# h and y of the later expert tiles on ScalarE alone, in an attention, expert and MLP kernel

## The chip, the cores and the metric

The kernel runs on one core of a Trainium2 chip. The metric is the device time of one execution in microseconds (us); of the kernel before, three runs are shown. One more execution was taken by the hardware profiler. Engines are named as in its rows: PE is TensorE (matmuls; PEld its weight loads), DVE is VectorE, ACT is ScalarE, POOL is GpSimd, SP is SyncE, which here issues DMAs. A name with a q (SPq, DVEq) is that engine's queue: instructions that issue DMAs, branch, or handle semaphores.

## The reference

Three stages follow one another, all in fp32: attention with a gated memory, a layer of eight experts of which each token takes one, and a dense MLP.

```python
def reference(...):                 # B,H,S,D = 4,8,576,64
    attn_out = g * mem_out + (1 - g) * softmax(q k^T / 8, causal) v
    x = attn_out.transpose(0, 2, 1, 3).reshape(B * S, H * D)      # 2304 x 512
    # experts: N,D,E,F = 2304,512,8,1024
    logits = x @ w_gate
    expert_idx = np.argmax(logits, axis=1)
    gate_w = softmax(logits)[arange(N), expert_idx]
    for e in range(E):
        mask = expert_idx == e
        h = np.maximum(x[mask] @ w1[e], 0.0)
        out[mask] = gate_w[mask, None] * (h @ w2[e])
    # dense MLP: 512 -> 2048 -> 512
    h = out @ w_in
    g = np.where(h > 0.0, h, np.exp(np.minimum(h, 0.0)) - 1.0)
    return g @ w_out
```

## The kernel before, in words

Every fp32 operand of a matmul is split into a high part (rounded to fp32r) and a low part (the rest); a product is three matmuls, high by high, low by high and high by low. So beside PE's work there is splitting work: a cast makes the high part, a subtraction the low part.

The stage that the change touches is the experts'. Tokens are sorted by expert into tiles of 128, and `mtile(t)` in `moe()` makes one tile. 23 tiles run (t = 0 to 22; two more stand behind an If and are not run here). The first four (`NE`) are made before the last batch of attention is routed; the tiles from t = 4 on are the ones that run one behind the other, with nothing of the attention beside them, from about 272 us to 517 us.

One tile does the following. POOL gathers the tokens (L1165). PE turns them (L1269), ACT and DVE split them (`split()`, high part L1190 on ACT or L1193 on DVE, low part L1196 on DVE). SP loads the expert's weights as four pieces of 1 MB (L1151), into one of two sets of buffers (`wraw` for even tiles, `wrbw` for odd ones); if the tile has the same expert as the tile that used that set before, an If skips load and split. `wsplit(k)` splits piece k: two casts of 128x1024 on ACT (`fh`, L1305) and two subtractions on DVE (`fl`, L1310). Pieces 0 and 1 are the first weight (names `wq` and `ws`), pieces 2 and 3 the second (`w`). 24 matmuls (L1330) make two halves of x w1 in two PSUM buffers. Then h = relu of the two halves: the first half on ACT (L1340), the second on ACT or DVE (L1343), as the setting `"re": [("ACT",), ("ACT", "DVE")]` allows. PE turns each half of h (L1355), ACT makes the high part of each turned half (`hh`, L1190), DVE the low part (`hl`, L1196). 24 matmuls (L1373) make y, and y times the gate is made on ACT (L1386) or DVE (L1389). POOL scatters y's rows to DRAM (L1415).

PE's order in one cycle is: the 24 L1330 of tile t, the turns of tile t+1's tokens (L1269), the turns of the first half of h of tile t (L1355), three L1373 of tile t-1, the turns of the second half, 21 L1373 of tile t-1, and then the L1330 of tile t+1. In the text a tile's cycle is counted from its first L1340 to that of the next tile.

Beside the tiles a piece of the MLP's preparation runs: the two dense weights are packed in 32 parts to a shorter form and stored in DRAM (`Widen.part`). A part is a load of 512 KB by SP into one of two `wide` buffers (L1102 or L1104), an absolute value on ACT (L1109), four packing steps on DVE (L1113, L1117, L1121, L1125), and a store to `wf` by SP (L1129). The load of part n+2 needs the buffer of part n, that is its L1125. The first piece that the MLP needs is read back from `wf` into the same `wide` buffers (L1431) and split there (high part on ACT, `raw0n<-wide`, low part on DVE).

The order on every engine's queue is set by a list scheduler (`Plan`, L116 to 258): each `pl.op(engines, costs, functions, r=..., w=..., prio=...)` is an operation with the keys that it reads and writes, and where two engines are given, the scheduler takes one of them by a table of costs and priorities. It simulates the engines with these costs, so another set of allowed engines or a further key moves operations that aren't named in the diff. What runs on the chip is then a fixed queue for each engine, in which an instruction that waits holds up all behind it.

Of the kernel before, what the change touches and what calls it, by code (L numbers as in the profile page):

```python
# [34 lines left out]
NE = 4  # L35
# [15 lines left out]
BOTH = ("DVE", "POOL")  # L51
# [437 lines left out]
def ca(n, sb=False, bias=False, acc=False):  # L489
    if acc:  # L490
        return 240 + 0.833 * n
    return (110 if sb else 65) + 0.833 * n


def cv(n):
    return 70 + 1.04 * n


def cv2(n):
    return 75 + 0.52 * n  # L500
# [6 lines left out]
def cpt(n):  # L507
    return 150 + 2.1 * n
# [660 lines left out]
def first_parts(c):  # L1169

    nc, pl, K = c.nc, c.pl, c.K
    wx, pr = Slot(c.rx), K["first"]

    def f():
        for cc in range(4):
            nc.tensor.transpose(wx.t[:, cc * P:(cc + 1) * P], c.ex[:, cc:DM:4], c.ident)
    pl.op("PE", 436, f, r=[c.se], w=[wx], prio=pr)
    xh, xl = [t.rearrange("p c n -> p (c n)") for t in c.x0]
    split(c, lambda: wx.t[:, 0:512], lambda: xh, lambda: xl, 512, [wx], "x0h", "x0l", pr, True, ("ACT", "DVE"), ("DVE",))
    for q in range(len(c.wq)):  # L1180
        hi, lo = c.wq[q]
        split(c, lambda q=q: c.wraw[0][0][:, 1024 * q:1024 * (q + 1)], lambda hi=hi: hi, lambda lo=lo: lo, 1024, [("raw", 0, 0)], ("hi", q), ("lo", q),
              pr + 10.0 * q, False, ("ACT", "DVE"), ("DVE",))


def split(c, src, hi, lo, n, rd, wh, wl, pr, psum, eh, el):
    nc, pl = c.nc, c.pl

    def ha():
        nc.scalar.copy(hi(), src())  # L1190

    def hv():
        nc.vector.tensor_copy(hi(), src())  # L1193

    def lv():
        nc.vector.tensor_sub(lo(), src(), hi().bitcast(F32))  # L1196

    def lp():
        nc.gpsimd.tensor_sub(lo(), src(), hi().bitcast(F32))
    he = {"ACT": (ca(n, sb=not psum), ha), "DVE": (cv(n) if psum else cv2(n), hv)}  # L1200
    le = {"DVE": (cv(n), lv), "POOL": (cpt(n), lp)}
    for es, d, r, w in ((eh, he, rd, wh), (el, le, rd + [wh], wl)):
        pl.op(es, [d[x][0] for x in es], [d[x][1] for x in es], r=r, w=[w], prio=pr, share=() if psum else BOTH)


def moe(tc, c, w1, w2, tiles):
    nc = tc.nc
    mp, pl, K = c.mp, c.pl, c.K
# [35 lines left out]
    def mtile(t):  # L1244
        pr = 1000.0 * t

        def at(x, y):
            return pr + y + K["moff"].get(f"{x}{t}", 0.0)
        rw = t % 2 if t < NTM else 1
        raw = c.wraw[rw]  # L1250
        part = t >= NE
        sg = Slot(r_xg)
# [21 lines left out]
        for _ in range(t > 0):  # L1274
            split(c, lambda: wx.t, lambda: xh.t.rearrange("p c n -> p (c n)"), lambda: xl.t.rearrange("p c n -> p (c n)"), 512,
                  [wx], xh, xl, at("xe", K["m_x"]), True, K["xe"], ("DVE",))

        flags = {}
        for e, eng in (("ACT", mybir.EngineType.Activation), ("DVE", mybir.EngineType.DVE)) if t else ():
            def mk(e, eng):  # L1280
                n = t - NE if part else t

                def f():
                    flags[e] = nc.values_load(c.R.sw[part][0:1, 1, n:n + 1], engines=[eng], min_val=0, max_val=1,
                                              skip_runtime_bounds_check_because="made on the chip as a flag")
                pl.op(e, 450, f, r=[("sw", part)], w=[("flag", e, t)], prio=at("f" + e, K["m_fl"]))
            mk(e, eng)

        def wsplit(k, pr):

            def src(q):
                return raw[k][:, 1024 * q:1024 * (q + 1)]
            keys = [[(x, 2 * k + q) for q in range(2)] for x in ("hi", "lo")]
            if not t:
                for q in range(2):
                    n = 2 * k + q
                    if n < len(c.wq):
                        continue
                    split(c, lambda q=q: src(q), lambda n=n: whi[n], lambda n=n: wlo[n], 1024, [("raw", rw, k)], keys[0][q], keys[1][q], at(f"w{n}t", pr - 1000.0 * t), False, K["wh"][n], K["wl"][n])
                return  # L1300

            def fh():
                with tc.If(flags["ACT"] < 1):
                    for q in range(2):
                        nc.scalar.copy(whi[2 * k + q], src(q))  # L1305

            def fl():
                with tc.If(flags["DVE"] < 1):
                    for q in range(2):
                        nc.vector.tensor_sub(wlo[2 * k + q], src(q), whi[2 * k + q].bitcast(F32))  # L1310
            ci = K["same"].get(t, (K["m_if"], K["m_if"]))
            pl.op("ACT", ci[0], fh, r=[("flag", "ACT", t), ("raw", rw, k)], w=keys[0], prio=at(f"sh{k}t", pr - 1000.0 * t))
            pl.op("DVE", ci[1], fl, r=[("flag", "DVE", t), ("raw", rw, k)] + keys[0], w=keys[1], prio=at(f"sl{k}t", pr - 1000.0 * t))

        def wparts(n):
# [2 lines left out]
        for cc in range(4):  # L1318
            def mk(cc):
                p1 = at("1t", K["m_1"] + 10 * cc)  # L1320
                if cc % 2 == 0:
                    wsplit(cc // 2, p1)
                (wh, wl), wk = wparts(cc)

                def mm(hfs, ns):
                    def f():
                        for hf in hfs:
                            for n in ns:
                                a, b = ((xh, wh), (xl, wh), (xh, wl))[n]
                                nc.tensor.matmul(g[hf].t, a.t[:, cc, :], b[:, 512 * hf:512 * (hf + 1)],  # L1330
                                                 start=(cc == 0 and n == 0), stop=(cc == 3 and n == 2))
                    return f
                for hf in range(2):
                    pl.op("PE", 3 * 216, mm((hf,), (0, 1, 2)), r=[xh, xl, *wk], w=[g[hf], ("tile", t)], prio=p1)
            mk(cc)
        sh = Slot(r_h)
        for hf in range(2):
            def mk(hf):
                def fa():
                    nc.scalar.activation(sh.t[:, 512 * hf:512 * (hf + 1)], g[hf].t, AF.Relu)  # L1340

                def fv():
                    nc.vector.tensor_scalar_max(sh.t[:, 512 * hf:512 * (hf + 1)], g[hf].t, 0.0)  # L1343
                es = K["re"][hf]
                pl.op(es, [{"ACT": ca(512), "DVE": cv(512)}[x] for x in es], [{"ACT": fa, "DVE": fv}[x] for x in es], r=[g[hf]], w=[(sh, hf)],
                      prio=at(f"r{hf}t", K["m_h"]))
            mk(hf)
        hs = []
        for k in range(2):
            def mk(k):  # L1350
                wt, hh, hl = Slot(rt), Slot(r_hh), Slot(r_hl)

                def f():
                    for j in range(4):
                        nc.tensor.transpose(wt.t[:, j * P:(j + 1) * P], sh.t[:, (4 * k + j) * P:(4 * k + j + 1) * P], c.ident)  # L1355
                pl.op("PE", 436, f, r=[(sh, k)], w=[wt], prio=at(f"h{k}t", K["m_h"]))
                split(c, lambda: wt.t, lambda: hh.t.rearrange("p c n -> p (c n)"), lambda: hl.t.rearrange("p c n -> p (c n)"), 512,
                      [wt], hh, hl, at(f"he{k}t", K["m_h"]), True, K["he"], ("DVE",))
                hs.append((hh, hl))
            mk(k)  # L1360

        y, sy = Slot(rg if t == NTM - 1 else ry), Slot(Ring("last", [c.wraw[0][0][:, 2 * XW:3 * XW]]) if t == NTM - 1 else r_y)
# [24 lines left out]

        def fv():
            nc.vector.tensor_scalar_mul(sy.t[:, 0:DM], y.t, sg.t[:, DM:DM + 1])  # L1389
        pl.op(("ACT", "DVE"), (ca(512), cv(512)), (fa, fv), r=[y, sg], w=[sy], prio=at("yt", 500))  # L1390

        if t < NE - NY:
            def f():
# [3 lines left out]
        if t < NE:  # L1397
            wy = Slot(rt)
            n = P * (t - NE + NY)
# [20 lines left out]
    for t in tiles:  # L1420
        mtile(t)
# [365 lines left out]
```

## Time and profile before

| | us |
|---|---|
| median of 3 runs | 928.09 (927.58 to 928.56) |
| profiled execution | 929.22 |
| its span, first to last instruction | 927.5 |
| PE busy | 894.7 (96%) |
| DVE busy | 601.5 (65%) |
| ACT busy | 372.0 (40%) |
| mean granted clock of PE | 0.989 |

The span is what the trace covers; the profiled execution's own time is 1.7 us longer. Busy times of the engines overlap. The page also cuts the span into 40 slices with the busy share of each engine in tenths; the experts' tiles stand in the slices 12 to 22, and PE's digit there is 9 in all but one. The clock of PE in that row is the share of full speed that was granted.

### The profile page before, as it was taken

To read this page: it belongs to the slowest core of one execution; us is meant where nothing else is said; L and a number is where in the kernel's file an instruction comes from. 1 tells how busy PE (TensorE), PEld (TensorE's weight loads), DVE (VectorE), ACT (ScalarE), POOL (GpSimd) and SP (SyncE) were. 2 spreads that over 40 slices of the span, in tenths; PEclk is the share of its full clock that TensorE was granted. 3 is DMA by queue.
4 is the path that set the end of the run, shared out by engine and by line. 5 is a ranking of instruction groups with operands and counts; after the bars stand their busy time and mean duration, and the time that the engine had idled before them with its cause. 6 is when DMAs were issued, how large, how long until landed. Compare 5 with 4: busy or idle time off the path is not lost. (4 is left out here: it accounts for less than half of the span.)

```text
span 927.5 us, 19069 instructions
## 1 busy us (share of the span) xinstructions
PE 894.7 (96%) x7404; PEld 742.9 (80%) x7404; DVE 601.5 (65%) x1093; ACT 372.0 (40%) x745; POOL 122.1 (13%) x176
## 2 busy tenths in 40 slices
PE   7999999999999999999989999999999999999996
PEld 4777778777788878887777899988888888888895
DVE  4889898989755787589996784444444444434442
ACT  5677777876432454246663431111111111111110
POOL 1111111121001132222221100010001000100100
PEclk9999999999999999999998999999999999999998
DMA  5444343357436964799984540110011000100000
GB/s 115 91 94 127 70 130 71 102 199 231 144 120 210 321 229 145 256 303 335 308 293 162 190 159 2 46 45 1 12 35 46 1 23 12 46 1 1 25 22 23
DMA packets 97108, 110.04 MB, mean 119 GB/s; under 512 B 65390, under 2 KB 65390, under 8 KB 94704
## 3 DMA queue, kind: packets, MB, share of 16 engines
q1 hardware_dynamic: 90992, 95.26, 32.5%
q0 software_dynamic: 4800, 13.18, 4.2%
q8 instruction: 59, 0.97, 0.4%
q10 hardware_dynamic: 1216, 0.30, 0.1%
q14 instruction: 41, 0.34, 0.1%
HBM read 87.94 MB, written 23.41 MB: 120 GB/s over the span
## 5 line engine op out<-in xcount | busy, mean ns | idle before, releaser
L1582 ACT ACTIVATE elu<-ptt 128x512 f32<-128x512 f32 x72 | 42.9, 597 | 316.5 <-PE ptt L1574 316.5
L1586 DVE TENSOR_SCALAR elu<-elu 128x512 f32<-128x512 f32 x72 | 31.0, 430 | 188.9 <-ACT elu L1582 188.9
L1599 PE MATMUL ptt<-w,gh 128*128 128x512 f32 x432 | 134.7, 393 | 0.0
L1373 PE MATMUL pmt<-w,hh 128*128 128x512 f32 x368 | 126.7, 406 | 0.0
L703 ACT ACTIVATE a<-pat,st 128x128 f32<-128x128 f32 (+3 forms) x144 | 78.0, 547 | 34.6 <-DVE st L698 27.3
L1599 PEld LDWEIGHTS ptt<-w,gh 128*128 128x128 f32 x432 | 79.3, 188 | 15.2
L1599 PE MATMUL ptt<-w,gl 128*128 128x512 f32 x216 | 84.2, 390 | 0.0
L1373 PEld LDWEIGHTS pmt<-w,hh 128*128 128x128 f32 x368 | 70.2, 191 | 14.0 <-DVE w L1310 0.3
L1373 PE MATMUL pmt<-w,hl 128*128 128x512 f32 x184 | 72.6, 394 | 0.0
L1574 PE MATMUL ptt<-yTh,w 128*128 128x256 f32 (+1 forms) x288 | 68.8, 318 | 0.0
L698 DVE TENSOR_REDUCE st<-pat 128x2 f32<-128x256 f32 (+4 forms) x80 | 64.4, 807 | 3.1 <-PE pat L690 1.4
L1488 DVE TENSOR_TENSOR gl<-tnh,gh 128x512 fp32r<-128x512 f32 x72 | 49.9, 693 | 4.7
L1590 DVE SCALAR_TENSOR_TENSOR tnh<-ptt,elu 128x512 f32<-128x512 f32 x72 | 49.8, 692 | 4.2
L820 POOL TENSOR_TENSOR raw<-ms,ls 128x80 f32<-128x80 f32 (+2 forms) x45 | 30.2, 694 | 169.1 <-DVE ls L808 161.7
L1574 PEld LDWEIGHTS ptt<-yTh,w 128*128 128x128 f32 x288 | 49.2, 190 | 3.9
L1599 PEld LDWEIGHTS ptt<-w,gl 128*128 128x128 f32 x216 | 40.5, 188 | 8.7
L676 PE MATMUL pat<-ab 64*128 64x128 f32 (+3 forms) x256 | 46.9, 474 | 0.0
L1574 PE MATMUL ptt<-yTl,w 128*128 128x256 f32 (+1 forms) x144 | 45.8, 318 | 0.0
L113 PE MATMUL pat<-ident,a 64*128 64x64 f32 x800 | 38.0, 233 | 7.1 <-ACT a L703 2.7
L1190 ACT CAST hh<-pmt 128x512 fp32r<-128x512 f32 x46 | 27.1, 589 | 43.4 <-PE pmt L1373 35.9
L1340 ACT ACTIVATE h<-pmt 128x512 f32<-128x512 f32 x29 | 17.3, 598 | 63.2 <-PE pmt L1330 61.6
L113 PEld LDWEIGHTS pat<-ident,a 64*128 64x128 f32 x800 | 30.6, 141 | 12.6 <-ACT a L703 5.9
(345 smaller groups left out, 1962.2 us busy)
## 6 DMA issues: line engine op xcount, KB each, us to landing
wraw<-in_moe_w_dram SPq DMA_DIRECT2D x24, 1024.0 KB
wrbw<-in_moe_w_dram SPq DMA_DIRECT2D x12, 1024.0 KB
wide<-in_moe_w_in_dram SPq DMA_DIRECT2D x16, 512.0 KB
wf<-half SPq DMA_DIRECT2D x32, 256.0 KB
wide<-in_moe_w_out_dram SPq DMA_DIRECT2D x16, 512.0 KB
wide<-wf SPq DMA_DIRECT2D x9, 512.0 KB
v<-in_v_dram SPq DMA_DIRECT2D x32, 128.0 KB
wraw<-yd SPq DMA_DIRECT2D x14, 258.0 KB
```

Of the source, the lines that this page charges most:

```text
L113: nc.tensor.transpose(out, x, ident[hs, hs])
L676: nc.tensor.matmul(s.t[:, 512 * h:512 * h + n], row(1)[hs, i * P:(i + 1) * P], row(0)[hs, 0:n], start=True, stop=False)
L698: nc.vector.tensor_reduce(ss.t[:, 2 * i:2 * i + (2 if i < 4 else 1)], src(), axis=AX.X if i < 4 else AX.XY, op=ALU.min)
L703: nc.scalar.activation(sa[i].t[:, h, :] if i < 4 else sa[4].t[:, 0:S].rearrange("p (y n) -> p y n", y=2), src()[:, h, :] if i < 4 else src ...
L820: e.tensor_tensor(o, a, b, op=ALU.add)
L1373: nc.tensor.matmul(y.t, a.t[:, 2 * (q % 2) + jj, :], b[:, 512 * jj:512 * (jj + 1)], start=(q == 0 and jj == 0 and n == 0), stop=(q == 3 an ...
L1488: nc.vector.tensor_sub(lo(), src(), hi().bitcast(F32))
L1574: nc.tensor.matmul(h.t[:, n * j + n0:n * j + n1], w(cc, a, ft), b(cc), start=(cc == 0 and x == 0), stop=(cc == 3 and x == 2))
L1582: nc.scalar.activation(se.t, h.t, AF.Exp)
L1586: nc.vector.tensor_scalar(se.t, se.t, 1.0, -1.0, op0=ALU.min, op1=ALU.add)
L1590: nc.vector.scalar_tensor_tensor(st.t, h.t, 0.0, se.t, op0=ALU.max, op1=ALU.add)
L1599: nc.tensor.matmul(acc[a].t, y.t[:, n * j + P * a:n * j + P * (a + 1)], wsub(1, k, ft // 2)[:, ft % 2, :], start=(ft == 0 and x == 0), sto ...
```

## The change

Three edits, all for the tiles from the fifth on (t >= NE = 4):

- both halves of h may be made by ACT only (before: the second half by ACT or DVE);
- y may be made by ACT only (before: ACT or DVE);
- the high parts of the turned halves write a further key ("he", k, t), and the ACT split of the second weight piece (`ws`, k = 1) of tile t reads the key of tile t-1's first half, so that the scheduler puts it behind that copy in ACT's queue.

`split()` takes the further keys as its argument `also`.

```diff
--- before.py
+++ after.py
@@ -1183,7 +1183,7 @@
               pr + 10.0 * q, False, ("ACT", "DVE"), ("DVE",))
 
 
-def split(c, src, hi, lo, n, rd, wh, wl, pr, psum, eh, el):
+def split(c, src, hi, lo, n, rd, wh, wl, pr, psum, eh, el, also=()):
     nc, pl = c.nc, c.pl
 
     def ha():
@@ -1199,8 +1199,8 @@
         nc.gpsimd.tensor_sub(lo(), src(), hi().bitcast(F32))
     he = {"ACT": (ca(n, sb=not psum), ha), "DVE": (cv(n) if psum else cv2(n), hv)}
     le = {"DVE": (cv(n), lv), "POOL": (cpt(n), lp)}
-    for es, d, r, w in ((eh, he, rd, wh), (el, le, rd + [wh], wl)):
-        pl.op(es, [d[x][0] for x in es], [d[x][1] for x in es], r=r, w=[w], prio=pr, share=() if psum else BOTH)
+    for es, d, r, w in ((eh, he, rd, [wh, *also]), (el, le, rd + [wh], [wl])):
+        pl.op(es, [d[x][0] for x in es], [d[x][1] for x in es], r=r, w=w, prio=pr, share=() if psum else BOTH)
 
 
 def moe(tc, c, w1, w2, tiles):
@@ -1309,7 +1309,7 @@
                     for q in range(2):
                         nc.vector.tensor_sub(wlo[2 * k + q], src(q), whi[2 * k + q].bitcast(F32))
             ci = K["same"].get(t, (K["m_if"], K["m_if"]))
-            pl.op("ACT", ci[0], fh, r=[("flag", "ACT", t), ("raw", rw, k)], w=keys[0], prio=at(f"sh{k}t", pr - 1000.0 * t))
+            pl.op("ACT", ci[0], fh, r=[("flag", "ACT", t), ("raw", rw, k)] + ([("he", 0, t - 1)] if k == 1 and t >= NE else []), w=keys[0], prio=at(f"sh{k}t", pr - 1000.0 * t))
             pl.op("DVE", ci[1], fl, r=[("flag", "DVE", t), ("raw", rw, k)] + keys[0], w=keys[1], prio=at(f"sl{k}t", pr - 1000.0 * t))
 
         def wparts(n):
@@ -1341,7 +1341,7 @@
 
                 def fv():
                     nc.vector.tensor_scalar_max(sh.t[:, 512 * hf:512 * (hf + 1)], g[hf].t, 0.0)
-                es = K["re"][hf]
+                es = K["re"][hf] if t < NE else ("ACT",)
                 pl.op(es, [{"ACT": ca(512), "DVE": cv(512)}[x] for x in es], [{"ACT": fa, "DVE": fv}[x] for x in es], r=[g[hf]], w=[(sh, hf)],
                       prio=at(f"r{hf}t", K["m_h"]))
             mk(hf)
@@ -1355,7 +1355,7 @@
                         nc.tensor.transpose(wt.t[:, j * P:(j + 1) * P], sh.t[:, (4 * k + j) * P:(4 * k + j + 1) * P], c.ident)
                 pl.op("PE", 436, f, r=[(sh, k)], w=[wt], prio=at(f"h{k}t", K["m_h"]))
                 split(c, lambda: wt.t, lambda: hh.t.rearrange("p c n -> p (c n)"), lambda: hl.t.rearrange("p c n -> p (c n)"), 512,
-                      [wt], hh, hl, at(f"he{k}t", K["m_h"]), True, K["he"], ("DVE",))
+                      [wt], hh, hl, at(f"he{k}t", K["m_h"]), True, K["he"], ("DVE",), [("he", k, t)])
                 hs.append((hh, hl))
             mk(k)
 
@@ -1387,7 +1387,8 @@
 
         def fv():
             nc.vector.tensor_scalar_mul(sy.t[:, 0:DM], y.t, sg.t[:, DM:DM + 1])
-        pl.op(("ACT", "DVE"), (ca(512), cv(512)), (fa, fv), r=[y, sg], w=[sy], prio=at("yt", 500))
+        es = ("ACT", "DVE") if t < NE else ("ACT",)
+        pl.op(es, [{"ACT": ca(512), "DVE": cv(512)}[x] for x in es], [{"ACT": fa, "DVE": fv}[x] for x in es], r=[y, sg], w=[sy], prio=at("yt", 500))
 
         if t < NE - NY:
             def f():
```

What the scheduler makes of it is seen in the queues. A first place is tile 21 (h_4053 is its h, wq and ws the pieces of the first weight of tiles 23 and 22, hh and x the high parts of h and of the next tokens). ACT's queue before:

```order
L1305 CAST wq_86<-wraw_77 128x1024
L1305 CAST wq_88<-wraw_77 128x1024
L1303 UNCONDITIONAL_BRANCH x2
L1109 ACTIVATE half<-wide_72 128x512
L1308 UNCONDITIONAL_BRANCH
L1340 ACTIVATE h_4053<-pmt_4152 128x512
L1303 COMPARE_AND_BRANCH
L1305 CAST ws_4167<-wraw_78 128x1024
```

DVE's queue before at the same place, up to the second half of h:

```order
L1310 TENSOR_TENSOR wq_87<-wraw_77,wq_86 128x1024
L1310 TENSOR_TENSOR wq_89<-wraw_77,wq_88 128x1024
L1308 UNCONDITIONAL_BRANCH x2
L1121 SCALAR_TENSOR_TENSOR half<-wide_71,half 128x512
L1113 TENSOR_SCALAR half<-half 128x512
L1125 SCALAR_TENSOR_TENSOR half<-wide_71,half 128x512
L1303 UNCONDITIONAL_BRANCH
L1343 TENSOR_SCALAR h_4053<-pmt_4153 128x512
L1308 COMPARE_AND_BRANCH
```

And ACT's queue now:

```order
L1305 CAST wq_86<-wraw_77 128x1024
L1305 CAST wq_88<-wraw_77 128x1024
L1303 UNCONDITIONAL_BRANCH x2
L1109 ACTIVATE half<-wide_72 128x512
L1308 UNCONDITIONAL_BRANCH
L1340 ACTIVATE h_4053<-pmt_4152 128x512
L1340 ACTIVATE h_4053<-pmt_4153 128x512
L1190 CAST x_84<-pmt_4151 128x512
L1190 CAST hh_4057<-pmt_4156 128x512
L1303 COMPARE_AND_BRANCH
```

Both halves of h now follow each other on ACT, and the second weight piece's casts, which stood between the first half and x, have moved behind the copy of the first turned half. DVE's L1343 is gone from its queue; the L1109 stands directly ahead of h as before, and it belongs to another part.

A second place is ACT's queue ahead of tile 18 (h_4049 is its h; wq the first weight piece of tile 20). Before:

```order
L1305 CAST wq_86<-wrbw_4113 128x1024
L1305 CAST wq_88<-wrbw_4113 128x1024
L1303 UNCONDITIONAL_BRANCH x2
L1109 ACTIVATE half<-wide_72 128x512
L1308 UNCONDITIONAL_BRANCH
L1340 ACTIVATE h_4049<-pmt_4154 128x512
L1303 COMPARE_AND_BRANCH
```

And now:

```order
L1305 CAST wq_86<-wrbw_4113 128x1024
L1305 CAST wq_88<-wrbw_4113 128x1024
L1303 UNCONDITIONAL_BRANCH x2
L1109 ACTIVATE half<-wide_72 128x512
L1308 UNCONDITIONAL_BRANCH
L1109 ACTIVATE half<-wide_71 128x512
L1340 ACTIVATE h_4049<-pmt_4154 128x512
L1340 ACTIVATE h_4049<-pmt_4155 128x512
```

Two L1109, of parts 25 and 26 in both `wide` buffers, now stand between the weight casts and the two halves of h; before it was one, and the second came after tile 18's h. In most other tiles one L1109 (in tile 17's the high part of the piece read back) stands directly ahead of the two halves, and ahead of the second half in tiles 8, 12 and 15. y (L1386) stands on ACT in each cycle between the casts of the third and the fourth weight piece. PE's own order is that of before, except that the turns of the first half stand three L1373 later in tiles 12 and 15; the order after the experts' stage is unchanged.

## Rows read from the trace of the kernel before

**Rows 1.** The page's busy time of each engine: us, share of the span, instructions.

```profile
PE 894.7 (96%) x7404; PEld 742.9 (80%) x7404; DVE 601.5 (65%) x1093; ACT 372.0 (40%) x745; POOL 122.1 (13%) x176
```

**Rows 2.** What PE waits for, 180 to 560 us: us in total, times, longest.

```profile
PE pmt L1355 <- DVE h L1343: 5.4, 2, 3.7
PE pmt L1355 <- DVEq L1308: 5.0, 3, 1.9
```

**Rows 3.** Table by stage: us, busy us of PE, PEld, DVE, ACT, POOL, clock, DMA share, GB/s.

```profile
340.28:354.68 14.40, 12.49 (x61) 10.24 (x60) 13.46 (x19) 7.17 (x10) 6.61 (x5) 1.00 0.44 140
354.68:391.50 36.82, 36.82 (x181) 30.98 (x180) 22.85 (x38) 10.04 (x17) 8.31 (x11) 1.00 0.61 205
...
428.60:442.64 14.04, 12.51 (x61) 10.24 (x60) 12.52 (x15) 9.61 (x13) 6.55 (x5) 1.00 0.89 303
442.64:456.75 14.11, 12.49 (x61) 10.25 (x60) 13.40 (x19) 6.82 (x9) 3.75 (x4) 1.00 0.87 311
...
469.04:483.04 14.00, 12.48 (x61) 10.24 (x60) 12.13 (x17) 9.72 (x13) 5.05 (x4) 1.00 0.66 221
...
483.04:501.81 18.77, 15.03 (x61) 12.19 (x60) 15.85 (x23) 5.77 (x8) 3.24 (x5) 0.82 0.72 250
```

**Rows 4.** Timeline of tile 21: start us, us, engine, line, operation, wait before it.

```profile
483.04 0.60 ACT L1340 ACTIVATE h<-pmt 128x512 f32<-128x512 f32 x1
...
484.48 2.36 DVE L1310 TENSOR_TENSOR wq<-wraw,wq 128x1024 fp32r<-128x1024 f32 x2
...
488.29 0.68 DVE L1343 TENSOR_SCALAR h<-pmt 128x512 f32<-128x512 f32 x1
...
489.03 1.11 PE L1355 MATMUL pmt<-ident,h 128*128 128x128 f32 x4 [3.74 <-DVE h L1343]
...
489.80 0.78 PE L1373 MATMUL pmt<-w,hh 128*128 128x512 f32 x1
...
496.85 2.88 PE L1330 MATMUL pmt<-wq,x 128*128 128x512 f32 x12
```

**Rows 5.** Timeline of PE in tile 10: first and next after its 21 second matmuls.

```profile
344.86 0.47 PE L1373 MATMUL pmt<-w,hh 128*128 128x512 f32 x1
...
349.72 0.39 PE L1330 MATMUL pmt<-wq,xh 128*128 128x512 f32 x1
```

**Rows 6.** Groups by line, 267 to 517 us: busy us, mean ns, idle before.

```profile
L1340 ACT ACTIVATE h<-pmt 128x512 f32<-128x512 f32 x21 | 12.5, 598 | 54.6 <-PE pmt L1330 53.2 <-issue 1.2
...
L1343 DVE TENSOR_SCALAR h<-pmt 128x512 f32<-128x512 f32 x17 | 11.7, 690 | 19.9 <-PE pmt L1330 19.0 <-DVEq L1308 0.5
...
L1386 ACT ACTIVATE wraw<-pmt,xs 128x512 f32<-128x512 f32 x1 | 0.7, 687 | 3.0 <-PE pmt L1373 3.0
...
L1109 ACT ACTIVATE half<-wide 128x512 f32<-128x512 f32 x30 | 20.2, 678 | 8.7 <-DMA wide<-in_moe_w_in_dram 4.5 <-DMA wide<-in_moe_w_out_dram 2.3 <-ACTq L1303 1.8
```

**Rows 7.** Timeline of tile 11, where ACT makes both halves of h.

```profile
354.68 1.31 ACT L1340 ACTIVATE h<-pmt 128x512 f32<-128x512 f32 x2 [2.54 <-PE pmt L1330]
...
355.64 0.60 PE L1355 MATMUL pmt<-ident,h 128*128 128x128 f32 x4
```

**Rows 8.** Timeline: loads into wide, the steps that waited, and the read-back's low part.

```profile
357.27 1.68 SPq L1104 DMA_DIRECT2D wide<-in_moe_w_out_dram  x1
...
362.36 0.67 ACT L1109 ACTIVATE half<-wide 128x512 f32<-128x512 f32 x1 [2.30 <-DMA wide<-in_moe_w_out_dram]
...
433.68 1.22 DVE L1196 TENSOR_TENSOR raw0n<-wide,raw0n 128x1024 fp32r<-128x1024 f32 x1
...
434.92 0.39 SPq L1102 DMA_DIRECT2D wide<-in_moe_w_in_dram  x1
...
446.96 0.68 ACT L1109 ACTIVATE half<-wide 128x512 f32<-128x512 f32 x1 [0.87 <-DMA wide<-in_moe_w_in_dram]
```

**Rows 9.** Timeline of ACT just before tile 21's h.

```profile
480.42 1.99 ACT L1305 CAST wq<-wraw 128x1024 fp32r<-128x1024 f32 x2
...
482.32 0.67 ACT L1109 ACTIVATE half<-wide 128x512 f32<-128x512 f32 x1
```

## The prediction

> **What bounds the kernel now.** I begin with the page's busy times: TensorE (PE) is at work for 894.7 us of the 927.5 [rows 1], so a change of work that sits on other engines can only pay where PE waits for them. Next I ask whom PE waits for while the expert tiles run (180 to 560 us). Two kinds of entry stand at the top, both at L1355, the transposes of h: 5.4 us in two waits for L1343, VectorE's (DVE's) copy of the second half of h, and 5.0 us in three waits named after L1308, the DVE queue's branch just ahead of that copy [rows 2]. That is five waits, 10.4 us, all for DVE's half of h.
>
> The table by stage shows where they are. One tile's cycle, from its first copy of h to the next tile's, takes 36.82 / 3 = 12.27 us where nothing waits, with PE busy in all of it. Five cycles are longer: 14.40 (tile 10), 14.04 (17), 14.11 (18), 14.00 (20) and 18.77 us (21) [rows 3]. Over 12.28 that is 2.12 + 1.76 + 1.83 + 1.72 + 6.49 = 13.92 us. The difference between 13.92 and 10.4 is the clock, mostly: in tile 21's cycle the granted clock falls to 0.82 on average, a mixture of 2.4 and 1.2 GHz.
>
> The timeline of tile 21 shows the mechanism. ScalarE (ACT) starts its half of h at 483.04. DVE starts the second half at 488.29, since a low part of the first weight piece (two L1310, 2.36 us) and three packing steps stand in front of it in its queue. PE stands 3.74 us, and after that its 21 second matmuls last from 489.80 to 496.85, 7.05 us [rows 4]; at tile 10, at full clock, the same 21 go from 344.86 to 349.72, 4.86 us [rows 5].
>
> **The change, part by part.** *h on ACT alone.* 17 copies of 690 ns leave DVE and come to ACT at 598 ns [rows 6]. Both halves now lie one behind the other on ACT. What that costs PE the trace already shows, as tile 11 is done so: the pair takes 1.31 us, PE turns the first half 0.96 us after its start, and the cycle belongs to the three that take 12.27 us each [rows 3, 7]. The second half is not needed until the first half is turned and three matmuls are done. So I put the serial copies at 0, and the gain at all five waits: -13.92 us. The clock's loss in tile 21 (7.05 - 4.86 = 2.19 us in the matmuls alone) is in it, because the 3.74 us stand before it goes.
>
> *The split of the second weight piece (L1305, `ws`) behind ACT's copy of the first turned half.* It moves back by two copies of h, x's copy and hh's, some 2 us. Its result is for the next tile, whose first matmuls begin 7.3 us into the cycle (below), and those on this piece later still. Behind 1.31 + 2 x 0.6 us of copies and its own 1.98 the split is over after about 5 us; it stays hidden, 0. If it were not moved, its 1.98 us would stand ahead of what PE's second matmuls need, so this part protects the gain and adds none.
>
> *y on ACT alone.* 19 multiplications by the gate leave DVE; ACT's one in this shape takes 687 ns [rows 6]. Nobody but the store of y waits for it; what counts is what stands behind it in ACT's queue. y is ready when the 21 matmuls end, 344.86 to 349.72, that is 9.44 us after tile 10's start at 340.28 or 9.44 - 2.12 = 7.3 us without its wait [rows 3, 5]. Behind y come two casts of the fourth weight piece and two of the first (1.99 us a pair), and sometimes a packing step (L1109, 0.67) [rows 6, 9]: 7.3 + 0.69 + 2 x 1.99 + 0.67 = 12.6 us, against a cycle of 12.28. All of them are real (not skipped by the If) only in the cycles of tiles 17 and 20, so h of tiles 18 and 21 starts late by about 0.4 us each; in tile 20's the queue is already without a gap before h [rows 4, 9]. I take 0.4 for tile 21, and less than the next term for tile 18.
>
> *ACT's packing steps move.* The order listing shows that L1109 now stands directly ahead of both copies of h in most tiles, twice before tile 18, and between the halves at three. L1109 waits for a load of 512 KB into one of two `wide` buffers. Where this load is late, h is late, and so is PE; before, an ACT wait there was harmless. The loads bound it. With light traffic one took 357.27 to 362.36, 5.1 us; with heavy traffic the one whose step is now the second before tile 18 took 434.92 to 446.96, 12.0 us [rows 8]. Its buffer is freed by DVE's low part of the piece read back from `wf` (1.22 us, [rows 8]). The cast ahead of that stands just before tile 17's h, so the load can go 1.2 us into that cycle, and the step must begin 0.67 us before its end: 12.28 - 0.67 - 1.22 = 10.4 us. The load is late by nothing (5.1) up to 1.6 us (12.0). I take 1.6, since it is the row of this very load. For the other steps ahead of h the time from freed buffer to step is 8 to 11 us, and I take 0 for them, as the waits of all 30 for their loads sum to only 4.5 + 2.3 us [rows 6].
>
> *The rest.* DVE loses some 25 us over the stage (17 and 19 operations of about 0.7) and gains nothing; its low parts come earlier. PE's order stays but for two tiles' transposes, and after the experts nothing is moved. 0, covered by PE's own 12.28 us per tile.
>
> **Sum.** -13.92 + 0.4 + 1.6 = -11.9 us. The profiled execution took 929.22 us (span 927.5), 1.1 above the median of 928.09. 929.22 - 11.9 = 917.3; on the scale of the medians, **916.2 us**. The bounds of the load term alone give 914.6 (no load late) and, with two more loads late by 1.6 each, 919.4.
>
> **Rivals.** *Loads late in many tiles.* Besides tile 18, the read-back ahead of tile 17's h and the steps ahead of tiles 10, 16, 19, 20 may wait. For it: the DMA engines are 0.9 busy around there, and one load needed 12.0 us. Against it: most loads were in time before. At four or five more places with 1.6 us each: 916.2 + 7 = about 923.
>
> *Slower.* The same waits, but long enough that the clock falls too: a wait of 3.74 us cost 6.49 us with the clock behind it [rows 3, 4]. A load must then come more than 14 us after its buffer is freed (10.4 + 3.7). Three such places make 3 x 6.49 = 19.5 us against the gain: 914.6 + 19.5 = 934. Against it: no load in the trace took 14 us.
>
> *Two copies in series cost after all.* If PE felt the second half everywhere, as serial halves end 598 ns later, 19 tiles would cost up to 19 x 0.6 = 11.4 us, which takes the gain back: 927.6, no change. Tile 11 speaks against it [rows 7]. The Trainium skill, page "TensorEngine Tiling (Array Packing)", section "PSUM Bottleneck", asks for just what is given up here: "Use both ScalarE and VectorE for PSUM evacuation". By that rule the sum would be about 0; by tile 11's row the rule does not hold where PE has work between the halves, and the row decides.
>
> *The wait is replaced.* DVE's low parts of the weights, not its h, might be what PE is short of next, with waits at L1330 or L1373 in the same five tiles: about 928. But PE shows no such wait among those listed [rows 2].
>
> **How the numbers follow.** A measurement can tell about 0.2%, 1.9 us. Forecast (914 to 919.5): 0.62. Many late loads (919.5 to 926): 0.22. Series or replaced wait (within 1.9 us of before): 0.07. Slower: 0.09, of which most is the clock's case. Faster is then 0.62 + 0.22 = 0.84, the same 0.07, slower 0.09. The range goes from 913.5, a little below the case without late loads, to 924, which takes in most of the second case; what lies above is some 0.2.
>
> **What would show it.** Right: the two entries at L1355 for DVE are gone, cycles of 12.28 us at tiles 10, 17, 20 and 21, a clock near 1.00 in tile 21's, ACT near 396 us busy and DVE near 575. A wait of PE of 1 to 2 us at tile 18, through ACT's L1109 and a `wide` load, shows the load term right; the same at several tiles shows the first rival; a stretch below 1.00 behind such a wait the second. Waits at L1355 of 0.5 us in every tile would show the series. The prediction is wrong if PE's waits sum to much over 4 us in this stage.

## The result, and the profile after

The changed kernel takes 917.43 us (median of 4 runs, 915.42 to 918.58), the kernel before 928.18 (4 runs, 927.58 to 928.56). The ratio is 0.9882 with a 95% interval of 0.9864 to 0.9901: about 11 us faster. The forecast was 916.2. Run a second time beside later experiments, the change gave 917.40 (0.9900, 0.9885 to 0.9915).

The page's busy times of the changed kernel, to be read against [rows 1]:

```profile
PE 890.9 (97%) x7404; PEld 741.0 (81%) x7404; DVE 580.0 (63%) x1060; ACT 391.3 (43%) x778; POOL 115.4 (13%) x176
```

33 instructions have gone from DVE to ACT: 17 for h and 18 for y (tile 22's y was on ACT before), less two casts (L1193, the high part of the tokens) which the scheduler now gives to DVE in turn. What PE waits for between 180 and 560 us (total, times, longest), against [rows 2]:

```profile
PE pmt L1355 <- ACT h L1340: 2.1, 3, 1.0
PE pmt L1269 <- DMA xs<-xd,r_tok: 1.0, 1, 1.0
```

Both entries for DVE's half of h are gone; a new one, for ACT's halves, is a fifth of their size. The table by stage, from h of one tile to h of the next, with the columns of [rows 3]; these are the cycles of tiles 10, 11, 15, 16, 17, 18, 20 and 21:

```profile
340.74:353.01 12.27, 12.27 (x61) 10.32 (x60) 10.75 (x16) 8.37 (x12) 3.17 (x3) 1.00 0.54 170
353.01:365.29 12.28, 12.28 (x61) 10.32 (x60) 6.61 (x11) 4.20 (x8) 2.27 (x3) 1.00 0.52 169
...
402.11:415.90 13.79, 13.39 (x67) 11.15 (x65) 11.42 (x17) 8.02 (x11) 3.76 (x4) 1.00 0.98 358
415.90:427.92 12.02, 11.38 (x54) 9.53 (x55) 11.68 (x16) 10.51 (x16) 3.27 (x3) 1.00 1.01 377
427.92:440.94 13.02, 13.02 (x66) 10.98 (x65) 10.59 (x12) 10.21 (x14) 3.07 (x4) 1.00 0.91 323
440.94:452.97 12.03, 11.74 (x57) 9.70 (x57) 11.14 (x16) 7.92 (x13) 2.45 (x3) 1.00 0.89 323
...
465.25:477.95 12.70, 12.70 (x63) 10.68 (x62) 11.16 (x16) 10.06 (x14) 1.19 (x1) 1.00 0.62 246
477.95:491.42 13.47, 13.35 (x64) 10.76 (x63) 11.28 (x16) 6.70 (x11) 1.63 (x4) 1.00 0.81 307
```

A window is bounded by ACT's copies, so a late h makes its own cycle start late: the window before it grows and the one behind it shrinks. Tile 10 is at PE's 12.27 us. The five windows that summed to 75.32 us sum to 63.49, the clock is at 1.00 in all, and the whole way from tile 4's h to tile 22's is 491.42 - 272.56 = 218.86 us where it was 501.81 - 272.10 = 229.71. These 10.85 us are the result: what stands ahead of that stage became 0.46 us longer, what stands behind it 0.50 us shorter.

Tile 21 at full clock: its 21 second matmuls run from 480.12 to 485.01 (start us, us, engine, line), 4.89 us as against 7.05 in [rows 4]:

```profile
480.12 0.48 PE L1373 MATMUL pmt<-w,hh 128*128 128x512 f32 x1
...
485.01 2.20 PE L1330 MATMUL pmt<-wq,x 128*128 128x512 f32 x9
```

What is left of PE's waits stands at tiles 16, 18 and 22. The timeline of each, from the load (SPq) over ACT's queue to PE:

```profile
405.41 0.39 SPq L1104 DMA_DIRECT2D wide<-in_moe_w_out_dram  x1
...
415.34 0.66 ACT L1109 ACTIVATE half<-wide 128x512 f32<-128x512 f32 x1 [2.12 <-DMA wide<-in_moe_w_out_dram]
415.90 1.07 ACT L1340 ACTIVATE h<-pmt 128x512 f32<-128x512 f32 x2
...
416.54 0.66 PE L1355 MATMUL pmt<-ident,h 128*128 128x128 f32 x4 [1.03 <-ACT h L1340]
...
429.12 1.98 SPq L1102 DMA_DIRECT2D wide<-in_moe_w_in_dram  x2
429.46 1.23 DVE L1196 TENSOR_TENSOR raw0n<-wide,raw0n 128x1024 fp32r<-128x1024 f32 x1 [0.23 <-DVEq L1308]
430.72 0.38 SPq L1102 DMA_DIRECT2D wide<-in_moe_w_in_dram  x1
...
439.79 1.26 ACT L1109 ACTIVATE half<-wide 128x512 f32<-128x512 f32 x2
440.94 1.09 ACT L1340 ACTIVATE h<-pmt 128x512 f32<-128x512 f32 x2
...
441.59 0.66 PE L1355 MATMUL pmt<-ident,h 128*128 128x128 f32 x4 [0.29 <-ACT h L1340]
...
483.46 0.38 SPq L1432 DMA_DIRECT2D wide<-wf  x1
...
490.47 1.05 ACT L1190 CAST wraw1n<-wide 128x1024 fp32r<-128x1024 f32 x1 [2.06 <-DMA wide<-wf]
...
492.07 1.15 PE L1355 MATMUL pmt<-ident,h 128*128 128x128 f32 x8 [0.77 <-ACT h L1340]
```

At tile 16 ACT waits 2.12 us for a load that took 9.9 us, with its L1109 directly ahead of h. At tile 22 it waits 2.06 us for the second piece read back from `wf`, whose cast stands ahead of h as well. At tile 18 no load is waited for: the two L1109 and y merely fill the queue. (The row at 429.12 merges two loads, those of parts 25 and 26; the second, at 430.72, is shown once more by itself.)

### The profile page after: what moved, and what is told of

It is laid out like the page before. It is cut to its first block, busy times and chain, and to the rows that moved or that the text cites. A ratio compares the mean times of both kernels' runs of the same rounds, so it can differ in the third digit from the quotient of the medians.

```text
span 916.6 us, 19073 instructions
## 1 busy us (share of the span) xinstructions
PE 890.9 (97%) x7404; PEld 741.0 (81%) x7404; DVE 580.0 (63%) x1060; ACT 391.3 (43%) x778; POOL 115.4 (13%) x176
## 4 chain that ended last, share of the span: by engine, by line
PE 51%; DMA 1%; ACT 1%; DVE 1%; issue 0%; POOLq 0%; POOL 0%; SPq 0%; ACTq 0%
PE ptt L1575 22%; PE ptt L1600 21%; PE pmt L1373 4%; PE pmt L1330 3%; PE ptt L1542 1%; DMA wide<-wf 1%; PE pmt L1355 1%; DVE wq L1310 0%; PE pmt L1269 0%; POOLq L1784 0%; ACT h L1340 0%; ACT wq L1305 0%; ACT wraw1n L1190 0%; ACT half L1109 0%; DVE half L1125 0%
## 5 line engine op out<-in xcount | busy, mean ns | idle before, releaser
L1373 PE MATMUL pmt<-w,hh 128*128 128x512 f32 x368 | 125.0, 401 | 0.0
L1373 PEld LDWEIGHTS pmt<-w,hh 128*128 128x128 f32 x368 | 69.1, 188 | 13.5 <-DVE w L1310 0.2
L1373 PE MATMUL pmt<-w,hl 128*128 128x512 f32 x184 | 71.8, 390 | 0.0
L1196 DVE TENSOR_TENSOR hl<-pmt,hh 128x512 fp32r<-128x512 f32 x46 | 31.6, 687 | 20.2 <-ACTq L1303 13.1
L1340 ACT ACTIVATE h<-pmt 128x512 f32<-128x512 f32 x46 | 27.0, 596 | 37.0 <-PE pmt L1330 35.7
```

The lines of the kernel that those rows point to most:

```text
L1373: nc.tensor.matmul(y.t, a.t[:, 2 * (q % 2) + jj, :], b[:, 512 * jj:512 * (jj + 1)], start=(q == 0 and jj == 0 and n == 0), stop=(q == 3 an ...
```

## The experiments

All ratios stand against the kernel before on the same chip; medians of different chips aren't to be compared. The stage is the time from tile 4's first copy of h to tile 22's in the profiled execution, which is a single one: in the change and in after_again, the same kernel, it differs by 1.4 us.

| kernel | median us | ratio | 95% interval | stage us |
|---|---|---|---|---|
| the change | 917.43 | 0.9882 | 0.9864 to 0.9901 | 218.9 |
| after_again | 917.40 | 0.9900 | 0.9885 to 0.9915 | 217.4 |
| h_key | 917.88 | 0.9895 | 0.9878 to 0.9912 | 217.9 |
| y_only | 922.79 | 0.9949 | 0.9932 to 0.9966 | 223.9 |
| h_y | 919.61 | 0.9915 | 0.9891 to 0.9938 | 220.1 |
| dve_first | 939.07 | 1.0128 | 1.0109 to 1.0147 | 235.1 |
| h_t21 | 926.91 | 0.9986 | 0.9973 to 1.0000 | 225.7 |
| after_t21_dve | 919.76 | 0.9923 | 0.9903 to 0.9942 | 218.7 |
| abs_dve | 922.58 | 0.9943 | 0.9929 to 0.9957 | 221.7 (*) |
| abs_dve_rb | 917.14 | 0.9886 | 0.9871 to 0.9902 | 216.1 (*) |
| behind_a | 920.15 | 0.9929 | 0.9916 to 0.9943 | 220.6 |
| behind_k | 922.10 | 0.9950 | 0.9936 to 0.9963 | 220.6 |
| mix_22_29 | 918.49 | 0.9906 | 0.9891 to 0.9922 | 218.6 |

(*) From tile 4's second copy: in these two its first copy is made 3.9 us ahead of the second, so their stage can't be read against the others. From tile 5's first copy to tile 22's they take 216.0 and 210.5 us, the change 212.1 and after_again 210.6.

**h_key: the change without its part on y.**

```diff
-        es = ("ACT", "DVE") if t < NE else ("ACT",)
+        es = ("ACT", "DVE")
```

> The change without its part on y: y may again be made by DVE, as before the change; both halves of h on ACT and the further key stay. Theory A (PE waited because DVE's half of h stood in DVE's queue behind a low part of a weight piece): the whole gain stays, 916 to 919 us, no wait of PE at L1355 for DVE. Theory B (DVE had too much to do, and any 0.7 us taken from it helps): about half of the work moved is back on DVE, so about half of the gain is lost, 921 to 923 us.

917.88 us, as the change within the intervals; PE's only wait for h is one of 1.5 us, for ACT. Theory A holds. Half of the work moved is back on DVE and nothing is lost, so it is not the amount of DVE's work that counted. The one wait again stands behind a load: ACT waits 4.54 us for an L1109 ahead of tile 20's h.

**y_only: y alone.**

```diff
-                es = K["re"][hf] if t < NE else ("ACT",)
+                es = K["re"][hf]
-...r=[("flag", "ACT", t), ("raw", rw, k)] + ([("he", 0, t - 1)] if k == 1 and t >= NE else [])
+...r=[("flag", "ACT", t), ("raw", rw, k)]
```

> The change's part on y alone: y of the tiles from the fifth on is made by ACT only, the second half of h stays with DVE, no further key. Theory A: the low parts of the weights still stand ahead of DVE's half of h, each wait of PE becomes shorter by y's 0.74 us at most, five times, 924 to 928 us, and tile 21's wait stays near 3 us or more. Theory B: as much work has left DVE as with h alone, so half of the gain comes, 922 to 923 us.

922.79 us, the gain of Theory B by its size, while the waits stay, as Theory A says. PE's waits in that kernel, as in [rows 2], and the cycle of tile 21, as in [rows 3]:

```profile
PE pmt L1355 <- DVE h L1343: 3.3, 2, 1.8
PE pmt L1355 <- DVEq L1308: 3.2, 3, 1.1
```

```profile
481.56:495.61 14.05, 12.00 (x58) 9.62 (x57) 11.73 (x18) 6.34 (x10) 2.19 (x4) 1.00 0.82 283
```

The same five waits are there, 6.5 us in place of 10.4, but they aren't shorter by y's 0.74 us each: tile 18's goes from 1.62 to 1.51, tile 21's from 3.74 to 1.77, the other three by 0.5 to 0.8, as the scheduler has moved other operations of DVE too. So Theory A's bound of 0.74 a wait was wrong, most of all at tile 21, where it expected 3 us or more. There the clock stays at 1.00, and its cycle is 4.72 us shorter (18.77 to 14.05), most of the 5.8 us by which the stage is shorter in the profiled executions; between the medians the gain is 4.8. h and y each shorten the same queue ahead of the same copy, and so their gains don't add up.

**h_y: the change without its further key.**

```diff
-...r=[("flag", "ACT", t), ("raw", rw, k)] + ([("he", 0, t - 1)] if k == 1 and t >= NE else [])
+...r=[("flag", "ACT", t), ("raw", rw, k)]
```

> The change without its further key: the casts of the second weight piece stand directly behind the two halves of h again, ahead of the copies of the turned halves. The prediction costs the key at nothing but says that it protects the gain. If the key matters, the casts' 1.98 us delay the copy of the first turned half in the seven tiles with new weights and PE waits for the buffer that it frees, up to 1 us each, 920 to 925 us. If it does not, as the turned half is only multiplied a cycle later, 916 to 919 us.

919.61 us; its interval overlaps the change's, so what the key is worth (0 to some 3 us) stays open. The trace shows no wait for the copies of the turned halves. Nor does the run test the key alone: without it the scheduler also gives 13 more casts of the tokens' high part to DVE. PE's two largest waits in that stage were at other places, for ACT's h of tile 20 and for the low part of x:

```profile
467.41 0.66 PE L1355 MATMUL pmt<-ident,h 128*128 128x128 f32 x4 [1.63 <-ACT h L1340]
...
487.67 2.56 PE L1330 MATMUL pmt<-wq,x 128*128 128x512 f32 x10 [1.01 <-DVE x L1196]
```

**dve_first: another repair, h stays on DVE.** From the kernel before:

```diff
-                es = K["re"][hf]
+                es = K["re"][hf] if t < NE or not hf else ("DVE",)
-..., r=[g[hf]], w=[(sh, hf)],
+..., r=[g[hf]], w=[(sh, hf), ("rh", hf, t)],
-            pl.op("DVE", ci[1], fl, r=[("flag", "DVE", t), ("raw", rw, k)] + keys[0], ...
+            pl.op("DVE", ci[1], fl, r=[...] + keys[0] + ([("rh", 1, t - 1)] if k == 0 and t > NE else []), ...
```

> The kernel before with another repair: the second half of h is made by DVE in every tile from the fifth on, and the low part of the first weight piece (L1310, wq) must stand behind it in DVE's queue. y as before. Theory A: the wait goes without any work moved to ACT, 914 to 919 us. Theory B: DVE has all its work and 21 halves of h more certain than before, 925 to 930 us. Theory C (two copies in series on ACT cost PE about 0.5 us a tile, and the change gained in spite of it): parallel copies are better still, below 912 us.

939.07 us, slower than before and outside all three theories. The timeline of tile 10 says why:

```profile
343.13 2.35 DVE L1310 TENSOR_TENSOR w<-wrbw,w 128x1024 fp32r<-128x1024 f32 x2
...
347.65 0.68 DVE L1343 TENSOR_SCALAR h<-pmt 128x512 f32<-128x512 f32 x1
...
348.38 0.66 PE L1355 MATMUL pmt<-ident,h 128*128 128x128 f32 x4 [3.15 <-DVEq L1308]
```

The key keeps the first weight piece's low part behind h; the second weight's low part (`w`, also 2.35 us) stands ahead of it, with four packing steps. The wait is not gone but longer: 8.8 us in three such waits for DVE's queue (tiles 10, 17 and 20), 1.9 in two more for DVE's h, and 4.8 in four for ACT, whose queue now meets late loads. These three tiles are the ones where it was `w` and not `wq` that stood ahead of h in the kernel before, too, as at tile 10:

```profile
339.50 2.35 DVE L1310 TENSOR_TENSOR w<-wrbw,w 128x1024 fp32r<-128x1024 f32 x2
341.77 0.68 DVE L1121 SCALAR_TENSOR_TENSOR half<-wide,half 128x512 uint32<-128x512 uint32 x1
342.49 0.69 DVE L1125 SCALAR_TENSOR_TENSOR half<-wide,half 128x512 uint32<-128x512 uint32 x1
343.69 0.69 DVE L1343 TENSOR_SCALAR h<-pmt 128x512 f32<-128x512 f32 x1 [0.52 <-DVEq L1308]
```

Only at tiles 18 and 21 was it `wq`, so the key aimed at the wrong piece in three places of five. (The `wq` in the queues ahead of tiles 18 and 21 is that of the next tile, 19 and 22: odd tiles load into `wrbw`, even ones into `wraw`.) The run shows that the half of h on DVE is as late as whatever the scheduler leaves ahead of it. Theory C finds no support: where nothing waits, a cycle with the halves side by side on ACT and DVE takes as long as one with both on ACT. This is tile 6's:

```profile
292.19:304.46 12.27, 12.27 (x61) 10.32 (x60) 6.69 (x11) 2.93 (x5) 2.43 (x3) 1.00 0.95 318
```

**h_t21 and after_t21_dve: one tile alone.** From the kernel before, and from the change:

```diff
-                es = K["re"][hf]
+                es = K["re"][hf] if t != 21 else ("ACT",)
```

```diff
-                es = K["re"][hf] if t < NE else ("ACT",)
+                es = ("DVE",) if t == 21 and hf else K["re"][hf] if t < NE else ("ACT",)
```

> The kernel before, with both halves of h on ACT in tile 21 alone. Theory A: the 6.49 us that tile 21's cycle is too long go, of which 3.7 us are the wait and the rest the fallen clock; the other four waits stay: 921 to 922.5 us. If the clock falls for another reason than this wait, 924 to 925 us, with a granted clock near 0.82 still in that cycle.

> The change, but the second half of tile 21's h is made by DVE again. In DVE's queue it stands behind the low part of the first weight piece (2.36 us) alone; y and the packing steps that stood there before are not ahead of it. Theory A: PE waits 1 to 2 us there, the clock does not fall, 918 to 919.5 us. If any copy by DVE brings back the whole of the tile's loss, 923 to 924 us.

The first gave 926.91 us, less gain than expected. Tile 21's cycle in the one and in the other:

```profile
483.42:498.17 14.75, 13.92 (x66) 11.00 (x64) 13.13 (x20) 5.78 (x9) 1.71 (x4) 1.00 0.76 259
```

```profile
476.12:490.65 14.53, 12.23 (x59) 9.93 (x59) 12.16 (x18) 6.58 (x10) 1.56 (x4) 1.00 0.88 308
...
480.40 0.66 PE L1355 MATMUL pmt<-ident,h 128*128 128x128 f32 x4 [2.30 <-DVE h L1343]
```

With h on ACT in tile 21 alone the clock is back at 1.00 and the cycle 4.0 us shorter, not 6.5: PE now waits 0.74 us for DVE's low part of x and 0.73 for ACT's h of tile 22. So the low part of x in the same DVE queue is late as well. The median gains only 1.7 us. The profiled execution (925.36 us) is near the shortest of the runs (925.12 to 928.69), and the loss that it is read against was a large one: the profiled execution of the kernel before had a mean granted clock of 0.989, while the 17 runs of that kernel beside h_t21 had 0.990 to 0.994, the three at 0.990 taking 929.3 to 931.1 us and the four at 0.994 taking 925.6 to 927.3. So the clock's part of the 6.49 us is probably not in every run. That this is why the median gains so little is not shown, as no other run of the kernel before was traced. In the change with that one copy back on DVE, PE waits 2.30 us and the clock does not fall: 919.76 us (0.9923), nearly as expected; its interval overlaps that of the change's second measurement (0.9900), so the price of this one copy is known from the wait in the trace and not from the time.

**abs_dve and abs_dve_rb: the packing's ACT step on DVE.** From the change; the second with one line more and a key that h writes (`rh`, as in dve_first):

```diff
-            nc.scalar.activation(o(), sd.t[:, :, 1].bitcast(F32), AF.Abs)
-        pl.op("ACT", ca(N, sb=True), f, r=[sd], w=w, prio=pr)
+            nc.vector.tensor_scalar(u(), sd.t[:, :, 1], 1, 1, op0=ALU.logical_shift_left, op1=ALU.logical_shift_right)
+        pl.op("DVE", cv(N), f, r=[sd], w=w, prio=pr)
```

```diff
-            split(c, src, ..., 1024, [sr], ("w0h", i), ...)
+            split(c, src, ..., 1024, [sr] + ([("rh", 1, 22)] if i else []), ("w0h", i), ...)
```

> The change, and the absolute value of the packing (L1109) made by DVE instead of ACT, as two shifts that clear the sign bit. Theory A: what is left of PE's waits for h (1.0 us at tile 16, 0.3 at tile 18, 0.8 at tile 22) comes from ACT standing in front of h for a late load; with L1109 gone from ACT the first two vanish and the read-back ahead of tile 22 stays, 915 to 916.5 us. Rival: DVE, which takes up 30 more operations of 0.4 to 0.7 us, becomes late with the low parts, 918 us or more, with waits of PE for DVE.

> As the kernel with the absolute value on DVE, and the cast of the second piece read back from wf must stand behind both halves of h of tile 22. Theory A: the last wait of PE for h (0.8 us, some 1.2 in the cycle) goes too, 914 to 915.5 us, unless the MLP's start then waits for this piece: in that case no gain over the kernel without it, 915 to 916.5 us.

In both the waits for h at tiles 16 and 18 are gone, as Theory A says. At tile 18 ACT's queue is too full by some 0.3 us: without the L1109, or without y (h_key), the wait goes. At tile 16 the second trace of the change (after_again, below) has no wait either, so there the cause rests on the timeline above. But the rival came true as well, at tile 21: the first kernel waits there for DVE's low part of x, its clock falls to 0.91 in that cycle, and at tile 22 it waits 2.09 us for h:

```profile
485.12 4.38 PE L1330 MATMUL pmt<-wq,x 128*128 128x512 f32 x11 [2.64 <-DVE x L1196]
```

In the second kernel that wait is 1.45 us, and the wait at tile 22 is gone. From tile 5 on it takes 210.5 us, as long as the change in its second trace (210.6), and its time, 917.14 us (0.9886), can't be told from the change's.

**behind_a and behind_k: the steps behind h instead.** From the change, with a key that h writes; for behind_a (behind_k: parts 27 and 29 behind h of tiles 19 and 20 too, and y free again):

```diff
+BEHIND = {23: 16, 25: 18, 26: 18}
-        pl.op("ACT", ca(N, sb=True), f, r=[sd], w=w, prio=pr)
+        pl.op("ACT", ca(N, sb=True), f, r=[sd] + ([("rh", 1, BEHIND[self.count])] if self.count in BEHIND else []), w=w, prio=pr)
```

The read-back's cast is behind h of tile 22 as above.

> The change itself once more, beside the two kernels below on the same chip: 916 to 918.5 us, with PE's waits for ACT's h at tile 16 (about 1 us), tile 18 (0.3) and tile 22 (0.8).

> The change, and the packing steps L1109 of parts 23, 25 and 26 and the cast of the second piece read back must stand behind both halves of h of tiles 16, 18 and 22; up to tile 15 the queues are those of the change. Theory A (what is left of the waits is a load that is late for a step of ACT that stands ahead of h): the waits at tiles 16, 18 and 22 go, 2.1 us and what follows them in the cycles (3.3 us in all), 914 to 915.5 us. If ACT's queue itself is too full there (y and both halves of h in it), tiles 16 and 18 still start late and it stays at 916.5 to 918 us.

> As the kernel with the moved steps, but y may again be made by DVE, and the steps of parts 27 and 29 are moved behind h of tiles 19 and 20 as well. Theory A: no wait of PE for h is left, 914 to 915.5 us, the same as with y on ACT, since y was never waited for. If y on DVE holds up the low parts of weights, 916 us or more with waits at L1330 or L1355 for DVE.

The change repeated itself in time, but not in its waits. What PE waits for ACT's h, in after_again:

```profile
PE pmt L1355 <- ACT h L1340: 0.7, 2, 0.4
```

These two are at tiles 18 and 22. At tile 16 ACT waits 0.69 us for the load, in place of 2.12, and PE not at all: how late a load is differs between two executions of one kernel. behind_a was slower, 920.15 us: the three waits are gone, and one of 3.02 us at tile 21 is new. (Its profiled execution, 925.11 us, is the longest of its six runs, the others being 918.85 to 921.07: what stands behind its stage is 4.0 us longer than in the change's trace, and the clock falls there once more.) Its timeline (three lines added, so L1112 is L1109, L1343 is L1340, L1358 is L1355):

```profile
461.13 0.39 SPq L1105 DMA_DIRECT2D wide<-in_moe_w_in_dram  x1
...
472.16 0.66 ACT L1112 ACTIVATE half<-wide 128x512 f32<-128x512 f32 x1 [5.00 <-DMA wide<-in_moe_w_in_dram]
...
480.06 0.67 ACT L1112 ACTIVATE half<-wide 128x512 f32<-128x512 f32 x1
480.63 1.07 ACT L1343 ACTIVATE h<-pmt 128x512 f32<-128x512 f32 x2
...
481.26 0.82 PE L1358 MATMUL pmt<-ident,h 128*128 128x128 f32 x4 [3.02 <-ACT h L1343]
```

A step that is made later frees its `wide` buffer later, and the load two parts on goes later. The load of part 29 takes 11.0 us here and ACT waits 5.00 us for it in the middle of tile 20, where the casts of both weights are queued behind it; h of tile 21 pays. behind_k (922.10 us) does the same one tile earlier (2.49 us at tile 20), against its Theory A; PE also waits 0.78 us there for DVE's y at tile 22, so y can be waited for. In these runs a wait that is taken from one place comes back at the next. That the chain of loads through two buffers is the limit fits them, but was not tested by itself.

**mix_22_29: the steps of the busy stretch alone on DVE.** From the change, abs_dve's step for parts 22 to 29 only, and the read-back behind h of tile 22:

```diff
+        self.count = getattr(self, "count", 0) + 1
+        if not 22 <= self.count <= 29:
             nc.scalar.activation(...)      # ACT
+        else:
+            nc.vector.tensor_scalar(...)   # DVE, as in abs_dve
```

> The change, with the absolute value of the parts 22 to 29 on DVE (two shifts), those before and behind on ACT, and the second read-back's cast behind h of tile 22; up to tile 14 the queues are those of the change. Theory A: the waits at tiles 16, 18 and 22 go, and as the first parts stay on ACT the stage does not start later, 913.5 to 915.5 us. Rival, which the moved steps have shown already (behind_a): a load that is late is late for the next engine too, and the wait comes back later, at tile 20 to 22, through DVE's low parts or through the last two L1109: 916.5 us or more.

918.49 us: the rival. Tiles 14 to 19 run without a wait, and tile 20 pays (six lines added: L1111 is L1109 on ACT, L1336 is L1330, L1361 is L1355):

```profile
472.99 0.50 PE L1336 MATMUL pmt<-wq,xl 128*128 128x512 f32 x1 [1.20 <-DVEq L1314]
474.28 0.68 ACT L1111 ACTIVATE half<-wide 128x512 f32<-128x512 f32 x1 [2.80 <-DMA wide<-in_moe_w_in_dram]
...
480.41 0.65 PE L1361 MATMUL pmt<-ident,h 128*128 128x128 f32 x4 [1.40 <-ACT h L1346]
```

No version beat the change by what can be measured. A third `wide` buffer, the direct test of the load chain, was not tried.

## Why the prediction was right, step by step

- **The five waits and the clock, -13.92 us.** Right. Both entries are gone, tile 10's cycle is 12.27, tile 21's clock 1.00 and its matmuls 4.89 us. That the place of DVE's half in its queue was the cause is shown by h_t21 (the wait gone at the one tile where the copy is moved) and by after_t21_dve (the wait back at the one tile where the copy is back); that it is the place and not DVE's load, by h_key beside y_only, which take about as much work from DVE and gain 9.7 and 4.8 us. What stood ahead was the low part of the first weight piece, as the prediction says of tile 21, at two tiles alone; at the other three it was the second weight's. The size rests on one execution with a low clock; in other runs of the kernel before the clock's share seems to be smaller (h_t21).
- **Serial copies at 0.** Right: with both halves on ACT a cycle takes 12.28 us (tile 11), as with one on each engine before. By the rule of the Trainium skill ("TensorEngine Tiling (Array Packing)", "PSUM Bottleneck": "Use both ScalarE and VectorE for PSUM evacuation") the sum would have been about 0; measured are -10.75 us. The page says this of matmuls that tiling has sped up, after which the copy "may become bottleneck"; here it isn't one: PE is busy for all 12.28 us of a cycle without a wait.
- **The key at 0, as protection.** Unsettled. Without it 919.61, with overlapping intervals, and not by the mechanism that the prediction gave: no wait for a copy of a turned half is in that trace.
- **y on ACT at a cost of 0.4 us and no gain.** The lateness is right: tile 20's cycle, counted between ACT's copies, is 12.70, 0.42 over 12.28. It cost PE nothing: PE is busy for all 12.70 us of that cycle, and the turns of h follow those of the next tokens without a gap, so this term should have been 0:

```profile
478.01 0.63 PE L1269 MATMUL pmt<-ident,xs 128*128 128x128 f32 x4
478.58 0.65 PE L1355 MATMUL pmt<-ident,h 128*128 128x128 f32 x4
```

  It is 18 copies of y that leave DVE, not 19, and not only the store waits for y (behind_k). That y has no share in the gain is wrong of y alone (y_only gains 4.8 us), and right as a term of this sum (h_key loses nothing without it).
- **A late load at tile 18, 1.6 us; 0 elsewhere.** The place was wrong, and that the size came near is luck. Part 26's load went out at 430.72, when DVE's low part of the piece read back was done: 2.8 us into tile 17's cycle and not 1.2. It was there in at most 9.7 us, not 12.0: its step ran at 440.37 without a wait, straight behind the step before it. The 0.29 us that PE waits at tile 18 are the queue's, the term that the prediction put below this one. The late ones were part 23 at tile 16 (9.9 us), a place that stands among the rivals alone, and the read-back ahead of tile 22, which the prediction did not list at all. From tile 4 to 22 the excess over the stage without the five waits (229.71 - 13.92 = 215.79) is 218.86 - 215.79 = 3.07 us, where the sum had 2.0.
- **The sum.** -11.9 forecast, -10.75 measured between the medians, -10.85 in the stage of the profiled executions: the missing 1.1 us is that last term, and no more than the 1.4 us by which the stage of the change differs between its two traces. The case "loads late in many tiles" happened at two places and cost a fraction of its 7 us.

## What to carry to other kernels

When PE waits for a short copy, look at what stands ahead of that copy in its engine's queue before asking how busy the engine is: 0.7 us of work waited behind 2.4 us that PE needed only later. Moving it to an engine that is idle at that moment was safer than a key in the scheduler, which held back one of the long operations that stood there and left the other (dve_first, 1.3% slower). And where a step that waits for a load stands ahead of the copy that PE needs, moving the step need not remove the lateness if the load's buffer is freed by that step: in behind_a, behind_k and mix_22_29 it came back a few tiles later.

## What the runs showed of the hardware that was not expected

The granted clock does not follow the longest wait alone. Before the change 3.74 us of standing at tile 21 was followed by 0.82 over the cycle, and in behind_a 3.02 us by 0.87 over the cycle behind it; but in dve_first 3.15 us at tile 10 left its cycle at 1.00, while 2.50 us at tile 17 left 0.90:

```profile
342.98:358.64 15.66, 12.51 (x61) 10.25 (x60) 14.69 (x21) 7.30 (x10) 5.04 (x4) 1.00 0.39 121
433.13:449.70 16.57, 14.07 (x61) 11.39 (x60) 13.40 (x17) 9.78 (x14) 5.92 (x5) 0.90 0.79 284
```

Beyond the wait itself the cycle lost 0.2 us at tile 10 of dve_first (15.66 - 12.28 - 3.15), 1.8 at its tile 17 and 2.75 at tile 21 before the change. What PE did before each of these was not compared, so what decides it stays open. Nor is the fall the same from run to run: the mean granted clock of the kernel before lies between 0.990 and 0.994 in its 17 runs beside h_t21, and the time goes with it (929.3 to 931.1 us at 0.990, 925.6 to 927.3 at 0.994).
